# GpSimd instead of ScalarE makes the three leading bits of the low words of all weight tiles

## The chip, the core and the metric

One core of a Trainium2 chip runs the program. Five engines work from queues of their own, each in its own fixed order: TensorE (PE in the profile, with its weight loads as PEld), VectorE (DVE), ScalarE (ACT), GpSimd (POOL) and SyncE (SP), whose queue issues all transfers here. They meet only at semaphores. The metric is the device time of one execution in microseconds (us); a comparison of two kernels rests on medians of several executions.

## What is computed

The reference is a gated linear attention followed by a feed-forward layer; cut to its core:

```python
# q, k, v, alpha: [4, 8, 768, 48], float32
for t in range(S):
    state = alpha[:, :, t, :, None] * state + einsum('bhd,bhe->bhde', k[:, :, t], v[:, :, t])
    y[:, :, t] = einsum('bhd,bhde->bhe', q[:, :, t], state)
x = y.transpose(0, 2, 1, 3).reshape(3072, 384)
h = x @ w_in                                  # w_in  [384, 2048], float64
g = h * erf(maximum(h, 0) + log1p(exp(-abs(h))))
out = (g @ w_out).astype(float32)             # w_out [2048, 384], float64
```

The two weight matrices come as float64, that is as pairs of 32-bit words in memory. [...]

## The kernel before

The tokens are cut into 24 attention chunks of 64 positions (two batch rows and all heads at a time) and into 12 feed-forward blocks of 256 tokens. A chunk goes through the steps `la`, `lq`, `lv` (loads) and `a1` to `a5` (running products of alpha, reciprocals, scores, state, output); two chunks fill the input of one block. A block goes through four groups of 512 hidden columns: `H` (first matmul, three passes in a split precision, line 429, and a copy of the result `hs`), `U`, `L1`, `L2`, `G`, `Z` (the nonlinearity, on ACT and DVE), `O` (second matmul, three passes, line 495, ahead of it the split of the activations into `gh` and `gl`), and `out`.

The weights stay in SBUF, each as a high part and a low part (`wi_hi`, `wi_lo`, `wo_hi`, `wo_lo`). `w_in` comes in 12 tiles of 128x512, `w_out` in 16 tiles of 128x384; each goes once through `weight()`, which takes these steps:

1. SP loads the tile with both words side by side into `wst` (line 522); the low words are every second 32-bit element.
2. The high word times 2^-112 gives `y`, the first half of the tile `wbuf` (line 530, through the helper at line 220 on ACT or 224 on DVE).
3. The three leading bits of the low word, as an integer from 0 to 7, give `z`, the second half of `wbuf` (line 532 on ACT, line 534 on DVE). This is what the change touches.
4. and 5. Two DVE operations shift `y` and join it with `z` and the sign (lines 536 and 540).
6. The rounded number goes into the high part (line 220).
7. The difference goes into the low part (DVE, line 554).

Everything is recorded in one order written out by hand, the string `SCHED`: each word of it takes the next step of one such sequence, and each engine gets its instructions in that order. The prefix `v:` before a word puts a step that may run on ACT or DVE on the other of the two: step 3 of a weight stands on ACT with it. It is there for 27 of the 28 tiles; for `wo_10` it is missing, and DVE makes the shift. `wst` and `wbuf`, as well as nearly all intermediate tiles, are drawn from one pool of 19 buffers (`big`), so a load or a step may have to wait until an older tile has been read. All weight work lies in the first quarter of the program. GpSimd only fills constants at the start.

Of the kernel before, what the change touches and what calls it, by code (L numbers as in the profile page):

```python
# [14 lines left out]
U32 = mybir.dt.uint32  # L15
AMIN = 1e-18
AF = mybir.ActivationFunctionType
ALU = mybir.AluOpType
# [129 lines left out]
def gla_moe(ctx: ExitStack, tc: tile.TileContext, qk, v, alpha, w_in, w_out, out):  # L148
    nc = tc.nc
# [33 lines left out]
    for i in range(NI):  # L183
        half = maskn[i * TC : (i + 1) * TC]
        nc.gpsimd.affine_select(
            out=half, in_=half, pattern=[[1, TC]], compare_op=ALU.is_ge, fill=0.0, base=0, channel_multiplier=-1
# [29 lines left out]
    on_vector = [False]  # L216

    def copy(out, in_, scale=1.0):
        if not on_vector[0]:
            nc.scalar.activation(out, in_, AF.Copy, scale=scale)  # L220
        elif scale == 1.0:
            nc.vector.tensor_copy(out=out, in_=in_)
        else:
            nc.vector.tensor_scalar(out=out, in0=in_, scalar1=scale, scalar2=None, op0=ALU.mult)
# [283 lines left out]
    def weight(hi, lo, src, n, by_pe):  # L508
        if src.dtype == F32:
            z = big.tile([P, n], F32, name="wst", tag="big")  # L510
            nc.sync.dma_start(out=z, in_=src)
            for _ in range(5):
                yield
            copy(hi, z)
            yield
            nc.vector.tensor_tensor(out=lo, in0=z, in1=hi.bitcast(F32), op=ALU.subtract)
            if by_pe:
                yield
            yield
            return  # L520
        st = big.tile([P, n, 2], I32, name="wst", tag="big")
        nc.sync.dma_start(out=st.rearrange("p n two -> p (n two)"), in_=src.bitcast(I32))
        yield
        low, high = st[:, :, 0], st[:, :, 1].bitcast(F32)
        buf = big.tile([P, 1024], F32, name="wbuf", tag="big")
        y, z = buf[:, :n], buf[:, 512 : 512 + n].bitcast(I32)
        sign = -1.0 if by_pe else 1.0
        copy(y, high, sign * 2.0**-112)
        top = y.bitcast(I32)
        yield  # L530
        if on_vector[0]:
            nc.scalar.activation(z, low.bitcast(U32), AF.Copy, scale=0.937 * 2.0**-29)  # L532
        else:
            nc.vector.tensor_scalar(out=z, in0=low, scalar1=29, scalar2=None, op0=ALU.logical_shift_right)
        yield
        nc.vector.scalar_tensor_tensor(
            out=z, in0=top, scalar=3, in1=z, op0=ALU.logical_shift_left, op1=ALU.bitwise_or
        )
        yield
        nc.vector.scalar_tensor_tensor(  # L540
            out=z, in0=top, scalar=-0x80000000, in1=z, op0=ALU.bitwise_and, op1=ALU.bitwise_or
        )
        yield
        z = z.bitcast(F32)
        copy(hi, z, sign)
        yield
        if by_pe:
            pl = ps_h.tile([P, 512], F32, name="pl", tag="h")
            nc.tensor.matmul(out=pl[:, :n], lhsT=ident, rhs=z, start=True, stop=False)
            nc.tensor.matmul(out=pl[:, :n], lhsT=ident, rhs=hi.bitcast(F32), start=False, stop=True)  # L550
            yield
            copy(lo, pl[:, :n], -1.0)
        else:
            nc.vector.tensor_tensor(out=lo, in0=z, in1=hi.bitcast(F32), op=ALU.subtract)
        yield

    def wi(n):
        c, kt = divmod(n, KT)
        cs = slice(c * 512, (c + 1) * 512)
        return weight(wi_hi[:, kt, cs], wi_lo[:, kt, cs], w_in[kt * P : (kt + 1) * P, cs], 512, n in WI_PE)  # L560

    def wo(f):
        return weight(wo_hi[:, f, :], wo_lo[:, f, :], w_out[f * P : (f + 1) * P, :], DM, f in WO_PE)
# [100 lines left out]
    with tc.manual_schedule():  # L664
# [4 lines left out]
        out=top[:, 0:2], in_=flags.rearrange("p n two -> p two n"), op=ALU.max, axis=mybir.AxisListType.X  # L669
# [80 lines left out]
```

## Time and profile before

| | us |
|---|---|
| median of 3 runs | 528.25 (526.23 to 528.33) |
| the profiled execution, device time | 526.75 |
| its span, first to last instruction | 525.0 |

The profile is of that one execution of 526.75 us, so 1.75 us of its time lie outside the span. The busy time of an engine counts the instructions that run, overlaps once; a PE that is busy need not run at its peak, since matmuls overlap and their ends are modelled. What an engine waited for stands behind an arrow as the idle time ahead of an instruction.

### The profile page before, as it was taken

To read this page: it belongs to the slowest core of one execution; us is meant where nothing else is said; L and a number is where in the kernel's file an instruction comes from. 1 tells how busy PE (TensorE), PEld (TensorE's weight loads), DVE (VectorE), ACT (ScalarE), POOL (GpSimd) and SP (SyncE) were. 2 spreads that over 40 slices of the span, in tenths; PEclk is the share of its full clock that TensorE was granted. 3 is DMA by queue.
4 is the path that set the end of the run, shared out by engine and by line. 5 is a ranking of instruction groups with operands and counts; after the bars stand their busy time and mean duration, and the time that the engine had idled before them with its cause. 6 is when DMAs were issued, how large, how long until landed. Compare 5 with 4: busy or idle time off the path is not lost.

```text
span 525.0 us, 16780 instructions
## 1 busy us (share of the span) xinstructions
PE 499.5 (95%) x7386; PEld 481.5 (92%) x7386; DVE 497.3 (95%) x715; ACT 485.1 (92%) x700; POOL 2.3 (0%) x14
## 2 busy tenths in 40 slices
PE   1699999999999999999999999999999999999994
PEld 1599999989999999999999999999999999999994
DVE  6999999999999999999999999999899999999993
ACT  6999999999999999989999899998898999999680
POOL 1000000000000000000000000000000000000000
PEclk9999999999999999999999999999999999999998
DMA  8976353341313203413012311123103120000001
GB/s 296 346 284 237 105 161 114 125 151 41 127 37 93 90 30 107 156 55 134 2 58 67 117 37 38 59 72 109 44 23 121 43 79 26 8 1 30 28 4 37
DMA packets 17936, 48.44 MB, mean 92 GB/s; under 512 B 1984, under 2 KB 5056, under 8 KB 17856
## 3 DMA queue, kind: packets, MB, share of 16 engines
q1 hardware_dynamic: 17856, 47.29, 26.6%
q8 instruction: 60, 0.98, 0.8%
q14 instruction: 20, 0.16, 0.1%
HBM read 42.57 MB, written 4.72 MB: 90 GB/s over the span
## 4 chain that ended last, share of the span: by engine, by line
PE 48%; ACT 25%; DVE 18%; issue 4%; DMA 3%; SPq 0%; DVEq 0%; ACTq 0%
PE acc L495 25%; PE ph L429 18%; ACT s L214 6%; ACT w L214 3%; ACT L213 3%; PE py L364 3%; ACT hs L220 3%; DVE t L458 2%; DVE gl L484 2%; ACT r L214 2%; DVE w L460 2%; DMA A<-in_alpha_dram 2%; ACT wbuf L220 2%; ACT wbuf L532 2%; DVE s L469 2%
## 5 line engine op out<-in xcount | busy, mean ns | idle before, releaser
L429 PE MATMUL ph<-x_hi,wi_hi 128*128 128x256 f32 x576 | 165.8, 288 | 1.8 <-ACT x_hi L220 1.1
L429 PE MATMUL ph<-x_lo,wi_hi 128*128 128x256 f32 x576 | 161.6, 281 | 1.1 <-issue 0.9
L429 PE MATMUL ph<-x_hi,wi_lo 128*128 128x256 f32 x576 | 161.3, 280 | 0.2 <-issue 0.2
L495 PE MATMUL acc<-wo_hi,gh 128*128 128x384 f32 x384 | 130.9, 341 | 0.0
L495 PE MATMUL acc<-wo_hi,gl 128*128 128x384 f32 x384 | 129.9, 338 | 0.8 <-DVE gl L484 0.6
L495 PE MATMUL acc<-wo_lo,gh 128*128 128x384 f32 x384 | 129.1, 336 | 0.0
L429 PEld LDWEIGHTS ph<-x_hi,wi_hi 128*128 128x128 f32 x576 | 109.0, 189 | 5.4 <-ACT hs L220 1.9
L429 PEld LDWEIGHTS ph<-x_hi,wi_lo 128*128 128x128 f32 x576 | 109.8, 191 | 1.0 <-issue 1.0
L429 PEld LDWEIGHTS ph<-x_lo,wi_hi 128*128 128x128 f32 x576 | 109.1, 189 | 0.6 <-DVE x_lo L395 0.5
L214 ACT ACTIVATE s<-s 128x1024 f32<-128x1024 f32 x96 | 100.1, 1054 | 6.2 <-DVE t L458 5.9
L495 PEld LDWEIGHTS acc<-wo_hi,gl 128*128 128x128 f32 x384 | 72.2, 188 | 2.6 <-DVE gl L484 2.4
L495 PEld LDWEIGHTS acc<-wo_hi,gh 128*128 128x128 f32 x384 | 72.2, 188 | 1.2
L495 PEld LDWEIGHTS acc<-wo_lo,gh 128*128 128x128 f32 x384 | 72.2, 188 | 0.0
L484 DVE TENSOR_TENSOR gl<-hs,gh 128x512 fp32r<-128x512 f32 x96 | 65.0, 689 | 6.5 <-ACT gh L220 1.7
L213 ACT ACT_TABLE_LOAD x52 | 66.7, 1283 | 0.9
L471 DVE SCALAR_TENSOR_TENSOR hs<-s,hs 128x1024 f32<-128x1024 f32 x48 | 58.6, 1222 | 0.7
L458 DVE TENSOR_TENSOR t<-s,w 128x1024 f32<-128x1024 f32 x48 | 58.2, 1219 | 1.0 <-ACT w L214 0.8
L469 DVE TENSOR_TENSOR s<-s,w 128x1024 f32<-128x1024 f32 x48 | 58.4, 1220 | 0.6
L460 DVE SCALAR_TENSOR_TENSOR w<-t,w 128x1024 f32<-128x1024 f32 x48 | 58.3, 1220 | 0.3
L220 ACT ACTIVATE hs<-ph 128x512 f32<-128x512 f32 x85 | 49.3, 590 | 3.3 <-PE ph L429 2.8
L214 ACT ACTIVATE w<-s 128x1024 f32<-128x1024 f32 x48 | 50.6, 1057 | 0.6
L214 ACT ACTIVATE s<-hs 128x1024 f32<-128x1024 f32 x48 | 50.4, 1058 | 0.4
(66 smaller groups left out, 719.3 us busy)
## 6 DMA issues: line engine op xcount, KB each, us to landing
kq<-in_qk_dram SPq DMA_DIRECT2D x24, 512.0 KB, 3.7
raw_v<-in_v_dram SPq DMA_DIRECT2D x24, 448.0 KB, 4.1
A<-in_alpha_dram SPq DMA_DIRECT2D x24, 260.0 KB, 3.3
wst<-in_moe_w_in_dram SPq DMA_DIRECT2D x12, 512.0 KB, 9.5
wst<-in_moe_w_out_dram SPq DMA_DIRECT2D x16, 384.0 KB, 3.5
out_dram<-o SPq DMA_DIRECT2D x24, 192.0 KB, 1.9
```

Of the source, the lines that this page charges most:

```text
L213: nc.scalar.preload_act_table_set(table)
L214: nc.scalar.activation(*args, **kw)
L220: nc.scalar.activation(out, in_, AF.Copy, scale=scale)
L364: nc.tensor.matmul(out=py[i][c0 : c0 + 32, kt, :], lhsT=left[r0 : r0 + rows, at0 : at0 + 32], rhs=right[r0 : r0 + rows, pair, i, :], start ...
L429: nc.tensor.matmul(out=o, lhsT=wt[:, kt, fs], rhs=xt[:, kt, :], start=n == 0, stop=n == 3 * KT - 1)
L458: nc.vector.tensor_tensor(out=t, in0=s, in1=w, op=ALU.mult)
L460: nc.vector.scalar_tensor_tensor(out=w, in0=t, scalar=2.0, in1=w, op0=ALU.add, op1=ALU.mult)
L469: nc.vector.tensor_tensor(out=s, in0=s, in1=w, op=ALU.mult)
L471: nc.vector.scalar_tensor_tensor(out=h, in0=s, scalar=RT2 / 2, in1=h, op0=ALU.subtract, op1=ALU.mult)
L484: nc.vector.tensor_tensor(out=gl.rearrange("p a t -> p (a t)"), in0=gg, in1=ghf.bitcast(F32), op=ALU.subtract)
L495: nc.tensor.matmul(out=self.acc[tt][:, :DM], lhsT=gt[:, u, ts], rhs=wt[:, f, :], start=f == 0 and n == 0, stop=f == NF - 1 and n == 2,)
L532: nc.scalar.activation(z, low.bitcast(U32), AF.Copy, scale=0.937 * 2.0**-29)
```

## The change

Step 3 of `weight()` is issued on GpSimd for all 28 tiles, as one multiplication with the same factor, read from and written to the same places. Neither ACT nor DVE makes it any more, and the prefix `v:` has no meaning for this step.

```diff
         yield
-        if on_vector[0]:
-            nc.scalar.activation(z, low.bitcast(U32), AF.Copy, scale=0.937 * 2.0**-29)
-        else:
-            nc.vector.tensor_scalar(out=z, in0=low, scalar1=29, scalar2=None, op0=ALU.logical_shift_right)
+        nc.gpsimd.tensor_scalar(
+            out=z, in0=low.bitcast(U32), scalar1=0.937 * 2.0**-29, scalar2=None, op0=ALU.mult
+        )
         yield
```

On ACT, the start of the program before reads as follows; `r` are attention tiles, `wbuf_129`, `wbuf_165` and `wbuf_173` belong to the first three weight tiles, and what stands in brackets is the semaphores that a row waits for:

```order
L220 ACTIVATE wbuf_129<-wst_127 128x512 [waits DMAHW4_49]
L532 ACTIVATE wbuf_129<-wst_127 128x512
L266 ACTIVATE r_137,flags_93<-A_109 128x512 [waits DVE_49,Activation_49]
L214 ACTIVATE r_137<-A_109 128x512 [waits Activation_49]
L214 ACTIVATE r_137,flags_93<-r_137 128x512 [waits Activation_49]
L220 ACTIVATE wbuf_165<-wst_139 128x512 [waits DMAHW6_49]
L532 ACTIVATE wbuf_165<-wst_139 128x512
L220 ACTIVATE wi_hi_98<-wbuf_129 128x512 [waits DVE_49]
L220 ACTIVATE wbuf_173<-wst_171 128x512 [waits DMAHW7_49]
L532 ACTIVATE wbuf_173<-wst_171 128x512
```

The same place on ACT in the changed kernel:

```order
L220 ACTIVATE wbuf_129<-wst_127 128x512 [waits DMAHW4_49]
L266 ACTIVATE r_137,flags_93<-A_109 128x512 [waits DVE_49,Activation_49]
L214 ACTIVATE r_137<-A_109 128x512 [waits Activation_49]
L214 ACTIVATE r_137,flags_93<-r_137 128x512 [waits Activation_49]
L220 ACTIVATE wbuf_165<-wst_139 128x512 [waits DMAHW6_49]
L220 ACTIVATE wi_hi_98<-wbuf_129 128x512 [waits DVE_49]
L220 ACTIVATE wbuf_173<-wst_171 128x512 [waits DMAHW7_49]
```

Only the rows of line 532 are gone; what is left keeps its order. On POOL, behind the constants, the changed kernel has 28 rows in a row, of which these are some from the start, the middle and the end:

```order
L531 TENSOR_SCALAR wbuf_129<-wst_127 128x512 [waits DMAHW4_49]
L531 TENSOR_SCALAR wbuf_165<-wst_139 128x512 [waits DMAHW6_49]
L531 TENSOR_SCALAR wbuf_173<-wst_171 128x512 [waits DMAHW7_49]
...
L531 TENSOR_SCALAR wbuf_389<-wst_387 128x512 [waits DMAHW7_49,Activation_49,Pool_49]
L531 TENSOR_SCALAR wbuf_442<-wst_438 128x512 [waits DMAHW1_49,Activation_49,Pool_49]
L531 TENSOR_SCALAR wbuf_495<-wst_489 128x512 [waits DMAHW3_49,DVE_49]
...
L531 TENSOR_SCALAR wbuf_1905<-wst_1903 128x384 [waits DMAHW3_49,DVE_49]
L531 TENSOR_SCALAR wbuf_2043<-wst_2041 128x384 [waits DMAHW5_49,DVE_49,Pool_49]
```

Each waits for its load, and from the ninth on also for the last readers of the buffer that `wbuf` takes over. On DVE the first join before, and what follows it:

```order
L536 SCALAR_TENSOR_TENSOR wbuf_129<-wbuf_129 128x512 [waits Activation_49]
L283 TENSOR_TENSOR kq_133<-kq_133,A_109 128x512 [waits DMAHW5_49]
L540 SCALAR_TENSOR_TENSOR wbuf_129<-wbuf_129 128x512 [waits DVE_49]
L273 TENSOR_TENSOR rw_143<-A_109,r_137 128x512 [waits Activation_49]
L328 TENSOR_TENSOR sT_162<-pS_145,maskn_87 128x512 [waits PE_49]
```

and in the changed kernel:

```order
L535 SCALAR_TENSOR_TENSOR wbuf_129<-wbuf_129 128x512 [waits Activation_49,Pool_49]
L283 TENSOR_TENSOR kq_133<-kq_133,A_109 128x512 [waits DMAHW5_49]
L539 SCALAR_TENSOR_TENSOR wbuf_129<-wbuf_129 128x512 [waits DVE_49]
L273 TENSOR_TENSOR rw_143<-A_109,r_137 128x512 [waits Activation_49]
L328 TENSOR_TENSOR sT_162<-pS_145,maskn_87 128x512 [waits PE_49]
```

The order of DVE stays, but for the one row of line 534 that it loses; the join now waits for POOL beside ACT. Behind the change in the file every line number is one lower.

## Rows read from the trace of the kernel before

**Rows 1.** The page: busy time of each engine over the span.

```profile
PE 499.5 (95%) x7386; PEld 481.5 (92%) x7386; DVE 497.3 (95%) x715; ACT 485.1 (92%) x700; POOL 2.3 (0%) x14
```

**Rows 2.** Stretches: length, busy time (instructions) per engine, clock, transfer share, GB/s.

```profile
9.00:26.00 17.00, 10.74 (x296) 9.00 (x296) 16.65 (x31) 16.42 (x36) 0.00 (x0) 1.00 0.95 359
26.00:122.00 96.00, 93.80 (x1723) 89.76 (x1724) 94.09 (x163) 95.02 (x175) 0.00 (x0) 1.00 0.48 162
122.00:468.00 346.00, 344.48 (x5054) 333.63 (x5053) 336.38 (x464) 332.10 (x443) 0.00 (x0) 1.00 0.20 67
...
10.00:99.00 89.00, 82.73 (x1575) 77.94 (x1576) 87.88 (x153) 88.41 (x166) 0.00 (x0) 1.00 0.59 206
99.00:122.00 23.00, 21.81 (x446) 20.81 (x445) 21.92 (x39) 22.25 (x43) 0.00 (x0) 1.00 0.40 129
```

**Rows 3.** The chain that ended last, in order: start, length, what.

```profile
12.49 0.56 ACT wbuf L220
13.04 0.55 ACT wbuf L532
...
98.19 1.15 DVE s L469
99.42 0.60 ACT hs L220
100.07 2.33 PE ph L429 x18
```

**Rows 4.** Groups of 9 to 122 us: busy, mean ns, idle before.

```profile
L532 ACT ACTIVATE wbuf<-wst 128x384 int32<-128x384 uint32 x15 | 8.4, 559 | 0.0
L532 ACT ACTIVATE wbuf<-wst 128x512 int32<-128x512 uint32 x12 | 8.1, 672 | 0.0
L220 ACT ACTIVATE wbuf<-wst 128x512 f32<-128x512 f32 x12 | 8.0, 670 | 0.8 <-DMA wst<-in_moe_w_in_dram 0.8
...
L328 DVE TENSOR_TENSOR sT<-pS,maskn 128x512 f32<-128x512 f32 x8 | 5.5, 684 | 0.0
L395 DVE TENSOR_TENSOR x_lo<-py,x_hi 128x192 fp32r<-128x192 f32 x16 | 5.4, 352 | 0.0
L323 DVE TENSOR_TENSOR T<-T,pu 128x192 f32<-128x192 f32 x12 | 3.7, 350 | 0.0
L222 DVE COPY hs<-ph 128x512 f32<-128x512 f32 x1 | 0.7, 691 | 0.0
L319 DVE SCALAR_TENSOR_TENSOR T<-pu,A 128x192 f32<-128x192 f32 x2 | 0.6, 350 | 0.0
L534 DVE TENSOR_SCALAR wbuf<-wst 128x384 int32<-128x384 int32 x1 | 0.4, 353 | 0.0
```

**Rows 5.** The first join (L536) among the instructions of 9 to 99 us.

```profile
L536 DVE SCALAR_TENSOR_TENSOR wbuf<-wbuf x23: 548/684/694, 10.5 to 93.8; 128x512 int32<-128x512 int32 x12, 128x384 int32<-128x384 int32 x11
```

**Rows 6.** All that POOL does with elements in the program (groups, mean ns).

```profile
L227 POOL MEMSET T<- 128x512 f32 x1 | 0.5, 524 | 0.0
L185 POOL TENSOR_SCALAR_AFFINE_SELECT maskn<-maskn 64x64 f32<-64x64 f32 x2 | 0.5, 235 | 0.1
masks.py:199 POOL TENSOR_SCALAR_AFFINE_SELECT ident<-ident 128x128 f32<-128x128 f32 x1 | 0.3, 292 | 0.1
```

**Rows 7.** DVE in order of time: start, length, what, idle before.

```profile
13.13 0.68 DVE L328 TENSOR_TENSOR sT<-pS,maskn 128x512 f32<-128x512 f32 x1
13.73 0.68 DVE L275 SCALAR_TENSOR_TENSOR rw<-rw,r 128x512 f32<-128x512 f32 x1
14.33 0.68 DVE L536 SCALAR_TENSOR_TENSOR wbuf<-wbuf 128x512 int32<-128x512 int32 x1
...
20.85 0.69 DVE L536 SCALAR_TENSOR_TENSOR wbuf<-wbuf 128x512 int32<-128x512 int32 x1 [0.15 <-ACT wbuf L532]
```

**Rows 8.** Who waited for whom from 9 to 122 us: total, times, longest.

```profile
PEld ph L429 <- ACT x_hi L220: 1.4, 1, 1.4
PEld ph L429 <- ACT hs L220: 1.0, 4, 0.5
PEld pu L307 <- ACT kn L220: 1.0, 1, 1.0
```

**Rows 9.** Whom SP's queue waited for up to 130 us: total, times, longest.

```profile
SPq L255 <- PE pu L307: 15.8, 4, 6.0
SPq L242 <- DVE T L325: 9.3, 1, 9.3
...
SPq L522 <- ACT wbuf L532: 0.4, 1, 0.4
```

## The prediction

> **What bounds the kernel now.** I read the busy times first [rows 1]: PE, DVE and ACT are all above 90% of the span, POOL is empty. No engine is idle enough to be dismissed, so the next view is the table of stretches [rows 2], because the change acts only while weights are made. From 10 to 99 us DVE is busy for 87.88 of 89.00 us and ACT for 88.41: both are full, with 1.12 and 0.59 us of idle time left. PE fills up later: between 9 and 26 us it works for 10.74 of 17.00 us, from 26 to 122 us for 93.80 of 96.00, and from 122 to 468 us for 344.48 of 346.00. What PE loses early it can't make up later; a delay of PE at 100 us is a delay of the end.
>
> The third view is the chain that ended last [rows 3]. In the weight stage it runs for long stretches through ACT, one instruction behind the other, and the instructions of line 532 that the change removes stand in it (13.04 us is one). That is the row that speaks for the change. But the chain passes through DVE too: at 98.19 us it is a DVE product, for which ACT's copy `hs` at 99.42 waits, and for that the first matmul at 100.07. So at 99 us a late DVE has no slack: what DVE loses before, less its own idle time, arrives at PE in full. The list of DVE's instructions [rows 7] shows the same close up: operations of 128x512 start every 0.60 us, and where DVE waits for the bits from ACT, the wait is 0.15 us.
>
> **What the change removes.** On ACT 27 instructions go: 12 of 672 ns and 15 of 559 ns, 8.1 + 8.4 = 16.5 us [rows 4]. On DVE the shift of `wo_10` goes, 0.35 us [rows 4]. If ACT alone bound the stage, this would be a gain of many us. It isn't alone: DVE's idle time from 10 to 99 us is 1.1 us [rows 2], and whatever ACT gives back, DVE can't run more than that ahead. Waits of PE for ACT in the stage are 1.4 + 1.0 + 1.0 = 3.4 us, for `x_hi`, `hs` and `kn` [rows 8]. So the gain side is between nothing and 3.4 us.
>
> **What it adds on POOL.** 28 instructions, 12 of 512 elements a partition and 16 of 384. No row shows this operation on POOL. The nearest rows are those that read and write [rows 6]: 292 ns for 128 elements and 235 ns for 64, so 0.89 ns for each further element; carried on, this gives 634 ns for 512 and 520 ns for 384. I take these, since the shape (one input, one output, all partitions) is the same. The bound below is a fill that only writes, 524 ns for 512 [rows 6] and three quarters of that, 393 ns, for 384. The bound above takes the whole 292 ns as proportional, 2.28 ns an element: 1168 and 876 ns. Even so POOL's own sum, 28 us at most, is small against 113 us; POOL isn't a bound by its load. The Trainium skill, page "GPSIMD Engine Reference", section "Elementwise — side-by-side cycle accounting", has 769 ns for 512 elements in a tight loop. By that figure the sum below would end some 2 us higher; no row here shows it.
>
> **The new wait.** The first join on DVE (L536 before, L535 after) now waits for POOL beside ACT. Queued behind it on DVE stand attention products, such as that of `kq` (L283), and the second join; ACT's copy into `wi_hi` and PE's scores wait for those. POOL needs only the landed tile and a free buffer, and ACT found both there in all but one case (0.8 us on a load [rows 4]). Before, the bits came after ACT's own copy of the high word; now the two run beside each other. A POOL instruction up to twice as long as ACT's is thus no later than ACT was, and I cost this wait at nothing. If POOL is kept from starting, the wait costs about the length of the instruction, which is the price of the next term in another place.
>
> **DVE beside POOL.** This decides. Both engines read and write the same memory, and no row shows DVE and POOL at work at the same time: POOL is done before DVE's first weight join. The bounds are far apart: nothing, if the two never meet, or the whole length of each POOL instruction taken from DVE, if one has to stand while the other reads. I take the upper end for the instructions of DVE that read two tiles from SBUF, because DVE streams without a gap from 10 us on [rows 2, 7], so POOL can find no free moment; that is a choice, and half or none of it is among the rivals. The Trainium skill, page "SBUF — State Buffer", section "Who interferes with whom", says that a DVE instruction with two SBUF inputs and a GpSimd instruction that reads SBUF contend, and that one blocks until the other is done. By that rule the price is the one taken; without it, nothing; no row of this trace can show which.
>
> The sum, up to 99 us, where DVE has no slack. By then 23 of the 28 joins are through, 12 of 512 and 11 of 384 elements [rows 5].
> - POOL: 12 x 0.634 + 11 x 0.520 = 13.3 us.
> - At each break DVE loses the overlap of neighbours: 0.69 us long, 0.60 us apart [rows 7], so 0.09 x 23 = 2.1 us. Together 15.4 us.
> - Some of DVE's instructions have at most one input in SBUF, the other in PSUM: L328, L395, L323, L222 and L319, 5.5 + 5.4 + 3.7 + 0.7 + 0.6 = 15.9 us [rows 4] of the 124.6 us that all groups of DVE add up to in that stretch, 13%. I let POOL run freely beside these: 15.4 x 0.87 = 13.4 us.
> - Off go the shift of `wo_10` (0.3) and DVE's idle time (1.1): 12.0 us.
>
> The five tiles after 99 us would cost 5 x 0.61 x 0.87 = 2.7 us, against 1.1 us that DVE is idle from 99 to 122 [rows 2]; up to 1.6 us more could come. I leave it out, since DVE and PE have some play there, and keep it in the range. SP's loads move with DVE: its queue waits for DVE and PE (9.3, 15.8 us) and hardly for line 532 (0.4) [rows 9], so an earlier ACT frees few buffers, and this term is nothing.
>
> Onto the profiled execution: 526.75 + 12.0 = 538.75, say **538.8 us**. It lies between the runs (526.23 to 528.33), 1.5 us under their median, so no shift is added; the range takes it in. With the bounds of POOL's length the same sum gives: below, 12 x 0.524 + 11 x 0.393 = 10.6, plus 2.1, times 0.87, less 1.4 = 9.7, or 536.4 us; above, 12 x 1.168 + 11 x 0.876 = 23.7, plus 2.1, times 0.87, less 1.4 = 21.0, or 547.8 us.
>
> **The rivals.**
> - *No meeting.* DVE runs as before, ACT is lighter. DVE then binds the stage, and the end moves by its idle time, at most 1.1 us, and the missing shift: 526.75 - 0.8 = about 526 us. For it speaks that ACT reads the same tiles beside DVE without a stretch in its durations; against it that this says nothing of POOL.
> - *ACT was the bound after all*, faster. The chain [rows 3] runs through ACT's copies to PE; with line 532 out of the way `x_hi`, `kn` and `hs` come earlier, and PE's 3.4 us of waits [rows 8] go: 523.4 us. This decides if POOL takes less than 3.4 / 23 = 0.15 us from DVE per instruction. Against it: DVE's 98% in that stretch.
> - *Half the price.* POOL reads partly while DVE is between inputs or in instructions that leave it room: 526.75 + 6 = 532.8 us.
> - *A slow POOL instruction.* 2.28 ns an element, for words that are every second one and change their type: 547.8 us. DVE's join would then also wait for POOL.
> - That the change doesn't do what it says can be put aside: ACT loses 27 instructions and POOL gains 28 in the built order, and nothing else moves.
>
> **How the numbers follow.** Chances: the sum as it stands 0.45, half the price 0.14, the slow instruction 0.10, no meeting 0.20, ACT the bound 0.11. The prediction is the likeliest, 538.8 us. The range goes from 525.6 to 548.0: its low end leaves out the faster case (0.11), its high end what is slower than the slow instruction's sum. Faster or slower by 0.5%, about what a measurement of this kernel can tell from no change, means under 525.6 or over 530.9 us. Slower: 0.45 + 0.14 + 0.10 = 0.69. Same: 0.20. Faster: 0.11.
>
> **What the profile after would show.** Right: POOL with 28 instructions, most between 9 and 110 us; ACT's busy time down by some 16 us and its idle time up; in the stretch of 10 to 99 us DVE's joins and products longer than 690 ns, or gaps ahead of L535 that end with POOL, 12 to 15 us in sum; PE less busy in the same stretch, by as much; from 130 us on the same picture as before, shifted. Wrong: DVE's products stay at 690 ns, 0.60 us apart, while POOL runs beside them; then the price taken for the meeting was none. Or POOL's instructions last far longer or shorter than 0.5 to 0.65 us; then the length was mis-sized. Or DVE is late at 99 us, and the end isn't; then PE had slack that I denied it.

## The result

| | us | ratio to before (95% interval) |
|---|---|---|
| before, median of 4 runs | 527.46 (526.23 to 528.33) | |
| changed, median of 4 runs | 533.37 (533.01 to 535.40) | 1.0122 (1.0086 to 1.0157) |

The changed kernel is slower by 1.2%, some 6 us. The profiled execution of it is the slowest of the four, 535.40 us with a span of 533.7; against that of before (526.75, 525.0) it is 8.65 us longer. Comparisons of traces below go by these two, comparisons of times by the medians.

The page of the changed kernel, against [rows 1], gives busy time, share and instructions:

```profile
PE 500.7 (94%) x7386; PEld 481.9 (90%) x7386; DVE 504.2 (94%) x714; ACT 474.2 (89%) x673; POOL 59.3 (11%) x42
```

ACT loses 27 instructions and 10.9 us of busy time; DVE loses one instruction and still gains 6.9 us; POOL shows 57 us more. Its stretches, against [rows 2] (length, busy time with instructions of PE, PEld, DVE, ACT, POOL, then clock, transfer share, GB/s):

```profile
9.00:26.00 17.00, 8.57 (x168) 7.19 (x168) 16.59 (x24) 10.25 (x22) 14.23 (x9) 1.00 0.77 305
26.00:122.00 96.00, 88.96 (x1792) 84.09 (x1794) 93.17 (x154) 83.59 (x145) 40.19 (x19) 1.00 0.50 163
122.00:468.00 346.00, 343.68 (x5072) 332.44 (x5059) 335.53 (x467) 329.94 (x449) 2.60 (x1) 1.00 0.22 69
10.00:99.00 89.00, 75.61 (x1519) 70.50 (x1520) 86.93 (x143) 71.86 (x133) 42.25 (x24) 1.00 0.57 197
```

From 10 to 99 us DVE is nearly as full as before and gets through 143 instructions instead of 153. ACT now has 17 us of idle time, where it had 0.6, and PE 13 us, where it had 6. From 122 us on the picture is that of before. So the loss arises in the weight stage, and on DVE. In order of time (start, length, engine, line, what; idle before it in brackets) the start of the stage, DVE and POOL, against [rows 7], reads:

```profile
9.08 2.01 POOL L531 TENSOR_SCALAR wbuf<-wst 128x512 int32<-128x512 uint32 x1 [5.98 <-DMA wst<-in_moe_w_in_dram]
9.73 1.02 DVE L278 TENSOR_TENSOR kq<-kq,rw 128x512 f32<-128x512 f32 x1
...
11.12 0.69 DVE L535 SCALAR_TENSOR_TENSOR wbuf<-wbuf 128x512 int32<-128x512 int32 x1 [0.37 <-POOL wbuf L531]
11.59 3.25 POOL L531 TENSOR_SCALAR wbuf<-wst 128x512 int32<-128x512 uint32 x2 [0.50 <-DMA wst<-in_moe_w_in_dram]
11.73 1.13 DVE L283 TENSOR_TENSOR kq<-kq,A 128x512 f32<-128x512 f32 x1
12.78 0.68 DVE L539 SCALAR_TENSOR_TENSOR wbuf<-wbuf 128x512 int32<-128x512 int32 x1
13.39 1.12 DVE L273 TENSOR_TENSOR rw<-A,r 128x512 f32<-128x512 f32 x1
14.43 0.68 DVE L328 TENSOR_TENSOR sT<-pS,maskn 128x512 f32<-128x512 f32 x1
```

The two engines meet, one read at a time: `kq` at 11.73 and `rw` at 13.39 take 1.13 and 1.12 us instead of 0.69, that is 0.44 us more for one POOL instruction each; the neighbours keep 0.68. So these two engines meet elsewhere than at semaphores too. The overlap of neighbours stays: the row behind `kq` starts 0.08 us before `kq` ends. Which kinds of instruction are stretched shows in the groups of DVE from 9 to 135 us (busy, mean ns):

```profile
L553 DVE TENSOR_TENSOR wi_lo<-wbuf,wi_hi 128x512 fp32r<-128x512 f32 x12 | 9.5, 821 | 0.0
L278 DVE TENSOR_TENSOR kq<-kq,rw 128x512 f32<-128x512 f32 x8 | 6.8, 847 | 0.0
L273 DVE TENSOR_TENSOR rw<-A,r 128x512 f32<-128x512 f32 x8 | 6.7, 833 | 0.0
L328 DVE TENSOR_TENSOR sT<-pS,maskn 128x512 f32<-128x512 f32 x8 | 5.5, 682 | 0.0
L224 DVE TENSOR_SCALAR wbuf<-wst 128x384 f32<-128x384 f32 x2 | 1.1, 539 | 0.0
```

The same groups before, where all but `sT` read nothing but SBUF:

```profile
L554 DVE TENSOR_TENSOR wi_lo<-wbuf,wi_hi 128x512 fp32r<-128x512 f32 x12 | 7.9, 683 | 0.0
L278 DVE TENSOR_TENSOR kq<-kq,rw 128x512 f32<-128x512 f32 x9 | 6.2, 688 | 0.1
L273 DVE TENSOR_TENSOR rw<-A,r 128x512 f32<-128x512 f32 x9 | 6.2, 690 | 1.5 <-ACT r L214 1.4
L224 DVE TENSOR_SCALAR wbuf<-wst 128x384 f32<-128x384 f32 x2 | 0.7, 358 | 0.0
```

`sT`, which reads one input from PSUM and had 684 [rows 4], has 682: it is left alone. Set side by side with the trace before, instruction by instruction, eleven of POOL's 12 reads of `w_in` make one DVE instruction longer, by 0.33 to 0.46 us. Of its 16 reads of `w_out`, seven do so by 0.29 to 0.35 us, three by 0.07, and six not at all. The read of `w_in` that is missing ran beside `sT`, and both kept their length:

```profile
25.23 1.53 POOL L531 TENSOR_SCALAR wbuf<-wst 128x512 int32<-128x512 uint32 x1
25.27 0.68 DVE L328 TENSOR_TENSOR sT<-pS,maskn 128x512 f32<-128x512 f32 x1
```

There is a second form of the same loss, a wait. Here is the stretch in which it is longest:

```profile
104.67 6.10 POOL L531 TENSOR_SCALAR wbuf<-wst 128x384 int32<-128x384 uint32 x1 [5.26 <-ACT s L214]
...
107.36 1.21 DVE L471 SCALAR_TENSOR_TENSOR hs<-s,hs 128x1024 f32<-128x1024 f32 x1
108.49 1.21 DVE L460 SCALAR_TENSOR_TENSOR w<-t,w 128x1024 f32<-128x1024 f32 x1
110.80 1.03 DVE L535 SCALAR_TENSOR_TENSOR wbuf<-wbuf 128x384 int32<-128x384 int32 x2 [1.10 <-POOL wbuf L531]
```

POOL's instruction starts at 104.67, DVE goes on without a gap and keeps its 1.21 us per instruction, and POOL ends at 110.77, only after DVE has run out of work at 109.70 and waits for just these bits. So POOL doesn't always get in between. What decides which engine goes first was not tested. Over the stage the waits that POOL causes (who waited for whom: us, times, longest) are:

```profile
DVE wbuf L535 <- POOL wbuf L531: 4.0, 5, 1.1
ACT w L214 <- POOL wbuf L531: 3.8, 3, 2.4
```

In the second, ACT wants to write a new tile into a buffer that POOL is still reading.

### The profile page after: what moved, and what is told of

The parts are those of the page before. It is cut to its first block, busy times and chain, and to the rows that moved or that the text cites. A ratio compares the mean times of both kernels' runs of the same rounds, so it can differ in the third digit from the quotient of the medians.

```text
span 533.7 us, 16828 instructions
## 1 busy us (share of the span) xinstructions
PE 500.7 (94%) x7386; PEld 481.9 (90%) x7386; DVE 504.2 (94%) x714; ACT 474.2 (89%) x673; POOL 59.3 (11%) x42
## 4 chain that ended last, share of the span: by engine, by line
PE 39%; DVE 29%; ACT 16%; issue 5%; DMA 3%; POOL 3%; SPq 0%; DVEq 0%; ACTq 0%; POOLq 0%
PE acc L495 20%; PE ph L429 15%; ACT s L214 4%; DVE w L460 4%; ACT w L214 3%; DVE t L458 3%; DVE gl L484 3%; DVE s L469 3%; POOL wbuf L531 3%; DVE hs L471 2%; DMA wst<-in_moe_w_out_dram 2%; ACT L213 2%; ACT hs L220 2%; PE py L364 2%; ACT r L214 1%
## 5 line engine op out<-in xcount | busy, mean ns | idle before, releaser
L531 POOL TENSOR_SCALAR wbuf<-wst 128x384 int32<-128x384 uint32 (+1 forms) x28 | 57.0, 2036 | 68.2 <-DMA wst<-in_moe_w_out_dram 42.3
```

Source lines behind the costliest of these rows:

```text
L531: nc.gpsimd.tensor_scalar(out=z, in0=low.bitcast(U32), scalar1=0.937 * 2.0**-29, scalar2=None, op0=ALU.mult)
```

## The experiments

Theory A: POOL's reading takes DVE's second input from it, and the loss is the time for which DVE stands. Theory B: the loss is the wait for a POOL instruction that is done late. Each run stands against the kernel before, run on the same chip.

**No reading.** POOL fills `z` with zeros in place of the multiplication (the three lowest bits of the weights are left out).

```diff
-        nc.gpsimd.tensor_scalar(
-            out=z, in0=low.bitcast(U32), scalar1=0.937 * 2.0**-29, scalar2=None, op0=ALU.mult
-        )
+        nc.gpsimd.memset(z, 0)
```

> The changed kernel with the POOL instruction replaced by a fill of the same place with zeros: it writes as many elements and DVE's join still waits for it, but it reads nothing (the three lowest bits of the weights are left out). Theory A (POOL's reading holds up DVE's second input): DVE's products are back at 690 ns each, DVE's busy time in the weight stage is that of the kernel before or under it, and the time is 525 to 528 us, at most 0.2% above the kernel before. Theory B (the loss is DVE's and ACT's waiting for a late POOL): the fills come early, so 526 to 529 us with DVE's instructions stretched as in the changed kernel if they were ever stretched by anything but POOL. Theory C (any POOL instruction disturbs DVE, writes too): DVE's products still take 800 ns and more on average, 531 to 533 us.

Measured: 524.95 us against 526.69, ratio 0.9962 (0.9948 to 0.9976). The same groups of DVE from 9 to 135 us:

```profile
L551 DVE TENSOR_TENSOR wi_lo<-wbuf,wi_hi 128x512 fp32r<-128x512 f32 x12 | 7.8, 678 | 0.0
L278 DVE TENSOR_TENSOR kq<-kq,rw 128x512 f32<-128x512 f32 x9 | 6.2, 684 | 0.1
L273 DVE TENSOR_TENSOR rw<-A,r 128x512 f32<-128x512 f32 x9 | 6.2, 684 | 0.8 <-ACT r L214 0.7
```

No stretch is left, though POOL writes as many elements and DVE's join waits for it as before. C falls: POOL's writing costs DVE nothing. And this is what the lighter ACT is worth, together with the shift of 0.35 us that DVE lost: 1.7 us, far from the 10.9 us that ACT saves. The time lies a little below the expected interval.

**Reading without relief and without a wait.** The kernel before, in which ACT makes the bits, and POOL reads the same words beside it into a tile that nobody reads.

```diff
+    scrap = const.tile([P, 512], I32, name="scrap")
...
+        nc.gpsimd.tensor_scalar(
+            out=scrap[:, :n], in0=low.bitcast(U32), scalar1=0.937 * 2.0**-29, scalar2=None, op0=ALU.mult
+        )
```

> The kernel before, in which ACT still makes the bits, with the POOL instruction added beside it: it reads the same words and writes a scrap tile that nobody reads. DVE waits for POOL nowhere; only the buffer of the words is held a little longer. Theory A (POOL's reading holds up DVE): DVE's busy time up by about 7 us as in the changed kernel, ACT not relieved, 532 to 538 us, ratio 1.008 to 1.020. Theory B (waiting for POOL): nothing waits, so 527 to 529 us, ratio under 1.004.

Measured: 536.53 us, ratio 1.0191 (1.0174 to 1.0208). The page:

```profile
PE 501.3 (94%) x7386; PEld 482.2 (90%) x7386; DVE 504.2 (94%) x715; ACT 486.3 (91%) x700; POOL 54.5 (10%) x42
```

DVE's busy time is up by the same 6.9 us as in the changed kernel, with nobody depending on the result. B as the main cause falls. As a smaller part waiting stays: three waits on a buffer that POOL still reads are left (1.5 and 1.2 us of ACT, 1.1 of DVE). Up to DVE's product `s` of the prediction, which stood at 98.11 us before, the two traces read (before, then this run):

```profile
10.00:98.11 88.11, 81.84 (x1568) 77.05 (x1569) 86.99 (x153) 87.52 (x164) 0.00 (x0) 1.00 0.60 208
10.00:106.37 96.37, 83.75 (x1573) 78.47 (x1574) 93.57 (x153) 89.22 (x166) 47.05 (x25) 1.00 0.54 190
```

The product is 8.26 us later: 6.58 us are longer instructions, 1.68 us more idle time of DVE. The largest pieces of idle time are the wait of 1.1 us for POOL and one of 1.4 us for ACT's bits, shortly after ACT had waited 1.5 us for POOL.

**Reading twice.** The changed kernel with a second such instruction behind the first.

> The changed kernel with a second POOL instruction for each tile, which reads the same words again and writes a scrap tile. Theory A: the stretch of DVE doubles, about 7 us more of DVE busy time than in the changed kernel, 538 to 544 us, ratio to the kernel before 1.020 to 1.032. Theory B: the bits are ready at the same time but the next tile's come later; 534 to 538 us, the growth standing in the idle time of DVE ahead of the join.

Measured: 552.88 us, ratio 1.0489 (1.0471 to 1.0506), above both expectations. DVE's busy time is 511.4 us, the further 7 us that A expected, but that is not all. Four stretches of 4 us (columns as above):

```profile
38.00:42.00 4.00, 2.35 (x18) 2.15 (x17) 0.00 (x0) 2.23 (x4) 3.76 (x4) 1.00 0.06 24
42.00:46.00 4.00, 0.66 (x16) 0.66 (x18) 3.04 (x4) 0.00 (x0) 3.84 (x3) 0.91 0.00 0
46.00:50.00 4.00, 4.00 (x65) 3.91 (x59) 2.60 (x4) 3.01 (x6) 3.84 (x3) 0.50 0.02 6
50.00:54.00 4.00, 3.18 (x132) 2.57 (x133) 3.94 (x8) 2.51 (x4) 3.77 (x3) 0.50 0.26 68
```

POOL is full there and has become the bound: DVE does nothing for 4 us, PE falls to 0.66 us of work in 4, and in the next 8 us its granted clock is 0.50 of full, the lower of its two levels. This run doubles more than the suspected cost, so it says only that the stretch grows with the reading.

**The same load on DVE itself.** The bits of all tiles by a shift on DVE, ACT relieved, POOL idle.

```diff
-        if on_vector[0]:
-            nc.scalar.activation(z, low.bitcast(U32), AF.Copy, scale=0.937 * 2.0**-29)
-        else:
-            nc.vector.tensor_scalar(out=z, in0=low, scalar1=29, scalar2=None, op0=ALU.logical_shift_right)
+        nc.vector.tensor_scalar(out=z, in0=low, scalar1=29, scalar2=None, op0=ALU.logical_shift_right)
```

> The kernel before with the bits of all 28 tiles made on DVE by a shift, as before for wo_10 alone; ACT is relieved as in the changed kernel, POOL idle. DVE gets 12 instructions of about 0.45 us and 15 of about 0.27 us start to start, 8 to 9.5 us. If a load on DVE in this stage arrives at the end undiminished (the step of the prediction at 99 us): 534 to 537 us, ratio 1.013 to 1.018. If half of it is absorbed by the lighter ACT: 530 to 532 us.

Measured: 533.98 us, ratio 1.0133 (1.0116 to 1.0150), at the low edge of the first interval. DVE's busy time is 505.3 us, 8.0 more than before, and the time 7.3 us more: a load on DVE in this stage arrives at the end nearly whole, wherever it comes from.

**Where it is lost.** POOL for the tiles of `w_in` alone, then for those of `w_out` alone; the other tiles stay as before.

```diff
+        if n == 512:     # the other run: n != 512
+            nc.gpsimd.tensor_scalar(out=z, in0=low.bitcast(U32), scalar1=0.937 * 2.0**-29, scalar2=None, op0=ALU.mult)
-        if on_vector[0]:
+        elif on_vector[0]:
```

> POOL makes the bits of the 12 tiles of w_in only (512 elements, 9 to 43 us); those of w_out stay as before. Theory A (price per read of about 0.44 us on DVE, where DVE is nearly without slack): 12 x 0.44 = 5.3 us less what ACT's relief gives back; 529 to 532 us, ratio 1.003 to 1.009. Theory B (waits for a late POOL, which stand mostly at the tiles of w_out): 527 to 528 us.

> POOL makes the bits of the 16 tiles of w_out only (384 elements, 45 to 125 us). Theory A: 16 x 0.33 = 5.3 us at most, about half of it seen as stretch in the changed kernel: 528 to 531 us, ratio 1.002 to 1.007. Theory B: 530 to 533 us, as most of the waiting (3.3 of 4.0 us of DVE, 3.8 us of ACT) stands here.

Measured: `w_in` 530.28 against 527.70 us, ratio 1.0049 (1.0032 to 1.0065); `w_out` 529.62, ratio 1.0043 (1.0028 to 1.0058). The two add up to 4.5 us of the 5.9. Their pages:

```profile
PE 498.7 (94%) x7386; PEld 480.1 (91%) x7386; DVE 501.1 (95%) x715; ACT 479.1 (91%) x688; POOL 22.9 (4%) x26
```

```profile
PE 498.1 (94%) x7386; PEld 479.4 (91%) x7386; DVE 499.1 (95%) x714; ACT 479.7 (91%) x685; POOL 39.5 (7%) x30
```

With `w_in` DVE's busy time is up by 3.8 us and it waits for POOL 0.4 us; with `w_out` it is up by 1.8 us, and here the waits stand: 2.2 us of DVE, 2.7 of ACT. So A carries the first half; in the second, stretch and waits share it. Neither part is worth having.

**The length of the POOL instruction.** Four of them at the start of the kernel before, where DVE has nothing to do: two of 512 and two of 384 elements, then (in another run) four of 512 in other forms.

```diff
+    words = big.tile([P, 1024], I32, name="words", tag="big")
+    bits = big.tile([P, 1024], I32, name="bits", tag="big")
+    nc.gpsimd.memset(words, 5)
+    for n in (512, 384, 512, 384):
+        nc.gpsimd.tensor_scalar(
+            out=bits[:, :n], in0=words[:, : 2 * n].rearrange("p (n two) -> p n two", two=2)[:, :, 0].bitcast(U32),
+            scalar1=0.937 * 2.0**-29, scalar2=None, op0=ALU.mult,
+        )
```

> The kernel before with four POOL instructions of the same form (two of 512, two of 384 elements, every second word of a filled tile) put among the constants at the start, where DVE does nothing. It shows the length of the instruction when nobody contends: if POOL's spans of 1.2 us and more in the changed kernel are its own length, 1.2 us and more here too; if they are waiting for DVE, 0.45 to 0.65 us here. The whole is 2 to 4 us longer for the late start; that time is not the question.

> The kernel before with four POOL instructions of 512 elements at the start, where DVE does nothing, in this order: whole words side by side as integers, every second word as integers, words side by side as float32, every second as float32. If the 1.51 us of the form in the changed kernel come from the step of two words, the first and third are under 1 us; if from the change of type, the third and fourth; if from neither, all four lie within 0.1 us of 1.5 us.

Each was run once, at 531.20 and 534.21 us; only the length of the instructions is read from them. The groups (busy, mean ns) of the first run, then of the second, where each group holds words side by side and every second word:

```profile
L183 POOL TENSOR_SCALAR bits<-words 128x512 int32<-128x512 uint32 x2 | 3.0, 1512 | 0.2
L183 POOL TENSOR_SCALAR bits<-words 128x384 int32<-128x384 uint32 x2 | 2.4, 1182 | 0.2
```

```profile
L186 POOL TENSOR_SCALAR bits<-words 128x512 int32<-128x512 uint32 x2 | 3.0, 1500 | 0.2
L186 POOL TENSOR_SCALAR bits<-words 128x512 f32<-128x512 f32 x2 | 3.0, 1498 | 0.1
```

Alone the instruction takes 1.51 and 1.18 us, 2.6 ns for each further element, whatever the type and the step. DVE stands for 0.44 us of this, under a third.

**What the hold goes by.** The added reading once more (against the run with reading but no relief), from words side by side, and from half of the words.

```diff
-            out=scrap[:, :n], in0=low.bitcast(U32), ...
+            out=scrap[:, :n], in0=st.rearrange("p n two -> p (n two)")[:, :n].bitcast(U32), ...
+            out=scrap[:, : n // 2], in0=low[:, : n // 2].bitcast(U32), ...     # the other run
```

> The kernel before with the added POOL instruction that reads the same number of words, but side by side, from the same tile, and writes a scrap tile. If DVE stands for as long as POOL reads elements: like the run with every second word, DVE's busy time up by 6 to 8 us, ratio 1.015 to 1.023. If it stands for the stretch of memory that POOL covers: half of that, ratio 1.006 to 1.012.

> The kernel before with the added POOL instruction reading only half of each tile's low words. If the hold on DVE goes by elements read: DVE's busy time up by 3 to 4 us, ratio 1.006 to 1.012. If it is a price per instruction (giving way and taking up again): as with the whole tile, ratio 1.016 to 1.022.

Side by side: 535.28 against 526.98 us, ratio 1.0141 (1.0117 to 1.0166), just under the expected interval, DVE's busy time again 504.2 us. So it isn't the stretch of memory. Half: 529.89 us, ratio 1.0054 (1.0039 to 1.0068), DVE's busy time 499.8 us, 2.5 more than before. Both figures lie under what was expected (3 to 4 us, 1.006 to 1.012), and far under those of the whole tile. A single stretched instruction, the first row, shows the hold:

```profile
23.41 0.90 DVE L541 SCALAR_TENSOR_TENSOR wbuf<-wbuf 128x512 int32<-128x512 int32 x1
24.23 0.68 DVE L545 SCALAR_TENSOR_TENSOR wbuf<-wbuf 128x512 int32<-128x512 int32 x1
```

0.90 instead of 0.68 us, so 0.22 us for 256 elements, half of the 0.44 for 512: the hold goes by elements, some 0.86 ns each, not by instructions. (With the words side by side a hold of 512 elements is a little shorter, 0.41 us.)

## Why the prediction was right, and what in it was not

The direction, the place and the mechanism came out as forecast, and 533.37 us lies in the range; the likeliest time, 538.8 us, was 5.4 us too high, and the change about half of the 12.0 us of the sum. What came closest is the rival "half the price", 532.8 us. The range, 525.6 to 548.0 us, took in all rivals but one, so that the time lies in it says little. That the sum came as near as it did is in part luck, since errors in it cancel, as the terms show.

*No slack at 99 us.* Right. DVE's product `s` that stood at 98.11 us before stands at 105.75 in the changed kernel, 7.64 us later, and the end of the span is 8.7 us later. Up to that instruction the changed kernel's row is:

```profile
10.00:105.75 95.75, 82.36 (x1570) 77.08 (x1571) 93.68 (x151) 77.97 (x141) 43.74 (x25) 1.00 0.55 190
```

Before, these were 88.11 us with 86.99 busy (the row stands with the second run above). So 6.7 us of the 7.64 are longer instructions, less the shift that DVE lost, and 0.95 is idle time. The sum had taken DVE's idle time of 1.1 us off, but it grew. The rest up to 8.7 us comes from the five tiles after 99 us, which the prediction kept in the range, and it comes as waits. Two rows of before and three of the changed kernel show it:

```profile
101.98 1.02 DVE L536 SCALAR_TENSOR_TENSOR wbuf<-wbuf 128x384 int32<-128x384 int32 x2
105.26 0.69 DVE L273 TENSOR_TENSOR rw<-A,r 128x512 f32<-128x512 f32 x1 [0.72 <-ACT r L214]
...
110.80 1.03 DVE L535 SCALAR_TENSOR_TENSOR wbuf<-wbuf 128x384 int32<-128x384 int32 x2 [1.10 <-POOL wbuf L531]
113.28 0.68 DVE L273 TENSOR_TENSOR rw<-A,r 128x512 f32<-128x512 f32 x1
128.33 0.56 DVE L535 SCALAR_TENSOR_TENSOR wbuf<-wbuf 128x384 int32<-128x384 int32 x1 [1.09 <-POOL wbuf L531]
```

The wait at 110.80 makes DVE 8.8 us late, but at 113.28 it is 8.0, because before DVE waited there for ACT and now does not. The last tile's wait, at 128.33, brings it to 8.7. The run with the shift on DVE shows the same step without POOL: 8.0 us of load, 7.3 us of time.

*The price of a meeting.* This is the term that was mis-sized. The sum took 0.634 and 0.520 us for POOL's instruction, all of it from DVE, and 0.09 us for the lost overlap. Both halves were wrong, in opposite directions. The instruction is longer, 1.51 and 1.18 us: the rows of the constants [rows 6] were the wrong neighbours (other operations, and one of them on 64 partitions, not on all), and the proportional bound, 1.168 and 0.876 us, was too short as well. And DVE stands for only 0.44 us of it (0.33 for 384 elements at the same 0.86 ns), not for the whole. That 0.44 comes near 0.634 is luck: the true length with the whole of it taken from DVE would have made the same sum 27.5 us, 554 us in all, far outside the range. The lost overlap, 2.1 us of the sum, was not lost at all.

With the measured price the sum up to 99 us is 12 x 0.44 + 11 x 0.33 = 8.9 us; 6.7 us were found, or 7.0 with the shift that DVE lost, some four fifths. The 13% that were let off were not far from the missing fifth, and in part for the right reason: the read at 25.23 ran beside `sT`. In part the reason is another, for some reads of `w_out` found DVE idle at the end of a wait, as the one of 4.95 us at 87.69, at whose end DVE had waited 1.09 us.

The Trainium skill, page "SBUF — State Buffer", section "Who interferes with whom", is borne out in who meets whom: two SBUF inputs against a reading POOL (847 ns for 688), not one input (682 for 684), not a POOL that only writes (684). Its word that the other blocks until the instruction is done is not: 0.44 of 1.51 us.

*The new wait at nothing.* Wrong in the small: 4.0 us of DVE's waiting ends with POOL. The reason given, that POOL could be up to twice as long as ACT, did not hold on two counts: alone POOL's 1.51 us are already more than twice ACT's 0.67, and POOL can be held up while DVE runs without a gap, as at 104.67. That ACT would wait for a buffer that POOL still reads (3.8 us) was not seen at all; the prediction thought of buffers for SP alone.

*What ACT gives back.* Right: 1.7 us in the run with the fill, between nothing and 3.4, the shift included. (The rival "no meeting" takes off 0.8 us, while its two terms, 1.1 and 0.35, can make up to 1.4; with that it would have stood at 525.3 us, under the range.) The 16.5 us were too much for ACT's load, though: neighbours on ACT overlap, and its busy time fell by 10.9. The rival "ACT was the bound after all" fell with it; the chain of before ran through ACT, but DVE stood right behind.

*The signs.* Up to 99 us DVE's longer instructions and its waits for POOL add up to about 9 us, against 12 to 15 forecast; ACT's busy time fell by 10.9 us, against 16; PE is less busy from 10 to 99 us by 7.1 us, about as much as DVE came late.

What stays open: by the medians the added reading costs 9.8 us and the changed kernel 5.9, while their profiled executions are longer by nearly the same, 9.0 and 8.7 us of span. The profiled execution of the changed kernel is 2 us above its median, and no trace of a quicker one is there to show what those 2 us are.

## What to carry to other kernels

An idle engine is not free room: ask which port or memory its work shares with the engine that bounds the stage. Two engines that are both full hide each other; before taking work off one, look at how much idle time the other has, for the relief can bring little more (here DVE had 1.1 us and lost an instruction of 0.35 us, and the gain was 1.7 us, not the 10.9 that ACT saved). A cheap way to part relief from collision is to let the new engine write without reading, or read for nobody.

## What the runs showed of the hardware

GpSimd's multiplication of 512 elements with a constant takes 1.50 us alone, as integers or float32, every word or every second one, some three times its fill of the same size, 0.52 us [rows 6]. While it reads, a DVE instruction with two inputs from SBUF stands for some 0.86 ns an element (0.44 us for 512, 0.22 for 256), and a DVE `TENSOR_SCALAR` from SBUF can be stretched too (539 ns on average for 358, above). The two engines do not simply take turns: one POOL instruction took 6.10 us and ended only after DVE had run out of work, while at 13.39 another held up a DVE instruction in the middle of an unbroken row.
